# Gate and value products of the first two token blocks made in two halves of 128 tokens

## The chip, the cores and the metric

The kernel runs on one core of a Trainium2 chip, with float32 data throughout. The metric is the device time of one launch in microseconds (us): from the inputs in HBM to the output in HBM. The time before is the median of three runs.

## The reference

The attention has 8 batches, 8 heads, 576 tokens each and a head width of 64. Every query keeps its 32 largest scores. The attention's output, with the heads side by side, is the input x (4608 tokens by 512) of a SwiGLU feed-forward block.

```python
scores = scale * np.matmul(q, k.transpose(0, 1, 3, 2))
kth = np.partition(scores, -top_k, axis=-1)[..., -top_k:-top_k + 1]
scores = np.where(scores >= kth, scores, -1000000000.0)
attn = np.exp(scores - np.max(scores, axis=-1, keepdims=True))
attn = attn / (np.sum(attn, axis=-1, keepdims=True) + 1e-09)
attn_out = np.matmul(attn, v)
x = attn_out.transpose(0, 2, 1, 3).reshape(B * S, H * D)      # (4608, 512)
g = x @ w_gate                                                # (4608, 1536)
silu = g * (1.0 / (1.0 + np.exp(-g)))
return silu * (x @ w_val) @ w_out                             # (4608, 512)
```

## The kernel before

**Units.** The attention is cut into 160 units: for each batch b (8), for each query tile qt (four of 128 queries and a last one of 64), for each pair of heads hp (4). Units with qt = 4 are "short": they work on one row of 576 scores for each partition, the others on two. In this text the units are numbered 0 to 159, so that units 0 to 3 make the first 128 tokens of batch 0, units 4 to 7 the next 128, and units 16 to 19 are the first short ones. The main loop runs over the units, and each turn of it issues a step of several units: for unit n the top-32 search on VectorE (`select`: MAX8, L271, and MATCH_REPLACE8, L275, in alternation, and a threshold, L281); for unit n-1 the addition of the penalty on GpSimd (`penalize`, L291 and L293) and the exponentials on ScalarE (`weigh`, L302); for unit n-2 the normalisation (`normalize`, L312, L314, L317); for unit n-3 the transposes on TensorE (`turn`, L329, copied out at L330); for unit n-4 the product with the values (`values`, L349 and L358, copied into the tile `xT` at L373); for unit n+1 the scores (`scores`, L250, copied out at L255).

**Feed-forward blocks.** The 4608 tokens are also cut into 18 blocks of 256 (`BLK`). `values` fills the tile `xT[kb]` of a block and counts in `done[kb]` the columns that are there, summed over the four head pairs. `feed(kb)` is a generator of the work of one block. It makes 12 products, a gate and a value product for each of six pairs of columns tiles of the weights: a product is eight matmuls into one PSUM tile "f" (three buffers), at L412, and each shows as two instructions in the trace, so 16. ScalarE empties a gate product with three operations (L430 to L432) and a value product with one (L437), and GpSimd multiplies (L433, L438). Then come 24 matmuls of the second layer (L449) into `o_ps`. The generator yields after half a product, or after two matmuls of the second layer; what lies between two yields is a "piece", and a block has 24 + 12 = 36 pieces.

**Order and credits.** The order of the instructions on each engine is the order in which the program issues them; nothing is rearranged. Pieces are put between the steps of the units by a ledger: each unit adds 4.6 credits (2.3 where it is short) up to a limit of 8, a piece costs one, and `pieces(2)`, `pieces(1)`, `pieces(1)`, `pieces(6)` in each turn of the loop are the places where pieces may be issued. `piece()` starts a new block only when all of its 256 tokens are there. The work that ScalarE and GpSimd do on a product is put off: it waits in the lists `on_act` and `on_pool` until two have gathered or the loop empties them.

**Weights.** The three weight matrices are loaded and rounded to a shorter mantissa in 72 portions of 128 by 256 (`rounded`, `weights`): a DMA, two ScalarE operations (L101, L106), two on GpSimd (L103, L113) and two on VectorE (L110, L116). A call of `next(weight)`, here a "weight step", issues four different portions' stages at once, five, three, two and no steps behind the newest. The loop calls for five steps to every eleven VectorE operations, which makes four or five steps in a full unit. `need(n)` makes sure that the first n portions have been issued before a matmul that uses them, and calls for as many steps on the spot as are missing. The first 48 portions are those of w_gate and w_val, eight for each pair of products; 24 portions of w_out follow.

```python
    def need(n):
        while ready[0] < n:
            next(weight)
```

Of the kernel before, what the change touches and what calls it, by code (L numbers as in the profile page):

```python
# [8 lines left out]
AF = mybir.ActivationFunctionType  # L9
ALU = mybir.AluOpType  # L10
FP32 = mybir.dt.float32
# [4 lines left out]
P = 128  # L16
# [4 lines left out]
BLK = 256  # L21
# [6 lines left out]
def kernel(  # L28
# [27 lines left out]
    nc = tc.nc  # L56
# [5 lines left out]
    NHP = H // 2  # L62
    KC = DM // P
    MC = DFF // P
    MS = MC // 2
    NBLK = B * S // BLK
    scale = 1.0 / float(D) ** 0.5
# [8 lines left out]
    ffn = ctx.enter_context(tc.tile_pool(name="ffn", bufs=2))  # L76
# [11 lines left out]
    wg = consts.tile([P, KC, DFF], FP32, name="wg")  # L88
    wv = consts.tile([P, KC, DFF], FP32, name="wv")
# [31 lines left out]
    def weights():  # L121

        pieces = []
        for f in range(0, DFF, WP):
            for src, dst in ((w_gate, wg), (w_val, wv)):
                for c in range(KC):
                    pieces.append((src[c * P : (c + 1) * P, f : f + WP], dst[:, c, f : f + WP]))
        for c in range(MC):
            for f in range(0, DM, WP):
                pieces.append((w_out[c * P : (c + 1) * P, f : f + WP], wo[:, c, f : f + WP]))  # L130
        pieces = [rounded(*p) for p in pieces]
        lags = (5, 3, 2, 0)
        for n in range(len(pieces) + lags[0]):
            for lag in lags:
                if 0 <= n - lag < len(pieces):
                    next(pieces[n - lag], None)
            ready[0] = max(n - lags[0] + 1, 0)
            yield
# [8 lines left out]
# [4 lines that stand above are left out]
# [187 lines left out]
    xT, done = {}, {}  # L338
# [41 lines left out]
    def store(o, g0):  # L380

        at = g0
        while at < g0 + P:
            b, c = divmod(at, S)
            j, p0 = divmod(c, P)
            n = min(g0 + P - at, S - c, P - p0)
            r0 = b * S + (c if j == J else J * p0 + j)
            dst = out[r0 : r0 + n, :] if j == J else out[r0 : r0 + J * (n - 1) + 1 : J, :]
            nc.sync.dma_start(dst, o[at - g0 : at - g0 + n, :])
            at += n  # L390

    on_act, on_pool = [], []

    def flush(queue):
        while queue:
            queue.pop(0)()

    def feed(kb):

        x = xT.pop(kb)
        hs = []

        def product(w, s, then):
            ps = ps_f.tile([P, 2, BLK], FP32, tag="f", name="f")
            need(8 * s + (4 if w is wg else 8))
            for i in range(2):
                m = 2 * s + i  # L410
                for kc in range(KC):
                    nc.tensor.matmul(  # L412
                        ps[:, i, :],
                        w[:, kc, m * P : (m + 1) * P],
                        x[:, kc, :],
                        start=(kc == 0),
                        stop=(kc == KC - 1),
                    )
                if i == 1:
                    on_act.append(lambda: then(ps))  # L420
                yield

        for s in range(MS):
            h = ffn.tile([P, 2, BLK], FP32, tag="h", name="h", bufs=MS + 1)
            hs.append(h)


            def gate(ps, h=h):
                half = ffn.tile([P, 2, BLK], FP32, tag="gv", name="half_g", bufs=3)
                nc.scalar.activation(h[:], ps[:], AF.Tanh, scale=0.5)  # L430
                nc.scalar.mul(half[:], ps[:], 0.5)
                nc.scalar.add(h[:], h[:], 1.0)  # L432
                on_pool.append(lambda: nc.gpsimd.tensor_mul(h[:], h[:], half[:]))  # L433

            def value(ps, h=h):
                val = ffn.tile([P, 2, BLK], FP32, tag="gv", name="val", bufs=3)
                nc.scalar.copy(val[:], ps[:])  # L437
                on_pool.append(lambda: nc.gpsimd.tensor_mul(h[:], h[:], val[:]))  # L438

            yield from product(wg, s, gate)  # L440
            yield from product(wv, s, value)
        for t in range(BLK // P):
            ps = ps_f.tile([P, DM], FP32, tag="f", name="o_ps")
            for m in range(MC):
                need(8 * MS + 2 * m + 2)
                if m == 6:
                    flush(on_act)
                    flush(on_pool)
                nc.tensor.matmul(  # L449
                    ps[:],  # L450
                    hs[m // 2][:, m % 2, t * P : (t + 1) * P],
                    wo[:, m, :],
                    start=(m == 0),
                    stop=(m == MC - 1),
                )
                if m == MC - 1:

                    def finish(ps=ps, t=t):
                        o = ffn.tile([P, DM], FP32, tag="o", name="o")
                        nc.scalar.copy(o[:], ps[:])  # L460
                        store(o, kb * BLK + t * P)

                    on_act.append(finish)
                if m % 2 == 1:
                    yield

    NU = len(units)
    todo = list(range(NBLK))
    current = []

    def piece():

        if len(on_act) > 1:
            flush(on_act)
        if len(on_pool) > 1:
            flush(on_pool)
        while True:
            if not current:
                if not todo or done.get(todo[0], 0) < NHP * BLK:
                    return False  # L480
                flush(on_act)
                flush(on_pool)
                current.append(feed(todo.pop(0)))
            if next(current[0], 0) == 0:
                current.pop()
                continue
            return True

    def fetch(n):

# [5 lines left out]
            load(i + NHP)  # L496

    def pieces(n):
        for _ in range(n):
            if credit[0] >= 1 and piece():  # L500
                credit[0] -= 1

    def run(steps):
        for _ in steps:
# [14 lines left out]
    credit = [0.0]  # L519
# [4 lines left out]
    for n in range(NU + VALUES):  # L524
# [37 lines left out]
        if n < NHP:  # L562
            load_v(n)
        pieces(2)
        flush(on_act)
        flush(on_pool)
# [12 lines left out]
    while piece():  # L579
        pass  # L580
# [48 lines left out]
```

## Time and profile before

| | |
|---|---|
| median of three runs | 1912.69 us (1911.77 to 1916.11) |
| profiled execution, its own time | 1915.14 us |
| span of that execution, first to last instruction | 1913.4 us |
| TensorE (PE) matmul busy | 1756.5 us, 92% |
| TensorE weight load (PEld) busy | 1297.0 us, 68% |
| VectorE (DVE) busy | 1608.9 us, 84% |
| ScalarE (ACT) busy | 1156.3 us, 60% |
| GpSimd (POOL) busy | 816.0 us, 43% |
| mean granted TensorE clock | 0.959 |

A row of the trace's groups gives the line of the program, the engine, the operation, the tiles (output, arrow, inputs), the shapes and the count, then the union of their busy time, the mean duration of one in ns, and the idle time of the engine before them with what ended it. In a timeline a row is a run of like instructions: its start in us from the span's start, its length, and in brackets the idle time before it. In a table by stretches, a row gives the busy time and the count of instructions of each engine in that stretch, then the granted TensorE clock as a share of full speed. Matmuls are pipelined, so that the distance between the starts of two is what one costs, and not its listed duration.

### The profile page before, as it was taken

The page shows a single profiled execution, that of the slowest core. Times are in us where ns is not written, and L with a number is a line of the kernel's source. Part 1 is how long each engine was busy: PE and PEld are TensorE (multiplying, and loading weights), DVE is VectorE, ACT ScalarE, POOL GpSimd, SP SyncE. Part 2 cuts the span into 40 slices and gives each one's busy share as a digit, 9 for nine tenths or more (in the row PEclk, how much of TensorE's full clock was granted, in tenths as well). Part 3 has the DMA queues.
Part 4 walks back from the last instruction along what each step waited for, and adds up shares of the span by engine and source line. Part 5 has one row for each costly group of instructions (what it writes and reads, how often), then busy time and mean ns, then how long its engine had stood idle before and what let it go on. Part 6 is the DMA issues. An engine that isn't in the chain of part 4 may idle for free.

```text
span 1913.4 us, 29363 instructions
## 1 busy us (share of the span) xinstructions
PE 1756.5 (92%) x10144; PEld 1297.0 (68%) x10144; DVE 1608.9 (84%) x3476; ACT 1156.3 (60%) x2821; POOL 816.0 (43%) x846
## 2 busy tenths in 40 slices
PE   3437789989999999999999999999999999999999
PEld 2336558667677777676768676868686868586866
DVE  7999889998899979998799979999799989999400
ACT  5656656566666656675657566656675656665421
POOL 4566644335343525353335343525243535353412
PEclk7668899989999999999999999999999999999999
DMA  7322202000300012000210003000210001000000
GB/s 185 88 78 82 67 22 69 11 1 3 76 12 12 2 27 63 12 1 13 53 37 1 12 4 87 1 12 1 60 31 12 1 14 45 18 1 12 1 12 11
DMA packets 111253, 59.58 MB, mean 31 GB/s; under 512 B 89088, under 2 KB 97280, under 8 KB 111104
## 3 DMA queue, kind: packets, MB, share of 16 engines
q1 hardware_dynamic: 109904, 57.41, 11.5%
q8 instruction: 80, 1.31, 0.3%
q14 instruction: 69, 0.57, 0.1%
q10 hardware_dynamic: 1200, 0.30, 0.1%
HBM read 48.23 MB, written 9.44 MB: 30 GB/s over the span
## 4 chain that ended last, share of the span: by engine, by line
PE 82%; DVE 6%; POOL 5%; ACT 4%; issue 2%; DMA 0%; SPq 0%; POOLq 0%; DVEq 0%; ACTq 0%
PE f L412 38%; PE o_ps L449 19%; PE av L358 8%; PE etps L329 7%; PE s L250 7%; DVE m L271 2%; POOL e L293 2%; DVE rest L275 2%; PE s L236 2%; ACT e L302 1%; PE av L349 1%; PE kqps L205 1%; ACT sc L255 1%; POOL size L113 1%; POOL size L103 1%
## 5 line engine op out<-in xcount | busy, mean ns | idle before, releaser
L271 DVE MAX8 m<-rest 128x8 f32<-128x576 f32 x864 | 615.2, 747 | 2.2
L275 DVE MATCH_REPLACE8 rest<-m,rest 128x576 f32<-128x576 f32 x576 | 424.1, 743 | 0.0
L412 PE MATMUL f<-xT,wg 128*128 128x256 f32 x1728 | 407.5, 386 | 0.0
L293 POOL TENSOR_TENSOR e<-e,sc 128x1152 f32<-128x1152 f32 (+1 forms) x160 | 382.7, 2392 | 42.4 <-DVE e L281 38.8
L412 PE MATMUL f<-xT,wv 128*128 128x256 f32 x1728 | 395.8, 381 | 0.0
L449 PE MATMUL o_ps<-wo,h 128*128 128x512 f32 x864 | 387.6, 598 | 0.0
L412 PEld LDWEIGHTS f<-xT,wg 128*128 128x128 f32 x1728 | 324.2, 191 | 71.5 <-issue 29.9
L412 PEld LDWEIGHTS f<-xT,wv 128*128 128x128 f32 x1728 | 325.3, 190 | 53.3 <-issue 10.5
L433 POOL TENSOR_TENSOR h<-h,half_g 128x512 f32<-128x512 f32 x108 | 138.4, 1282 | 453.0 <-ACT h L432 435.0
L271 DVE MAX8 m<-sc 128x8 f32<-128x576 f32 x288 | 205.6, 750 | 123.9 <-ACT sc L255 78.8
L329 PE MATMUL etps<-ident,e 128*128 128x128 f32 (+1 forms) x1312 | 187.5, 288 | 125.9 <-POOL size L103 48.1
L449 PEld LDWEIGHTS o_ps<-wo,h 128*128 128x128 f32 x864 | 159.4, 190 | 193.1 <-issue 186.9
L329 PEld LDWEIGHTS etps<-ident,e 128*128 128x128 f32 (+1 forms) x1312 | 159.4, 147 | 176.1 <-POOL size L103 51.3
L330 ACT COPY et<-etps 128x512 f32<-128x512 f32 (+1 forms) x448 | 184.7, 482 | 148.5 <-PE etps L329 147.1
L302 ACT ACTIVATE e<-e,bias 128x576 f32<-128x576 f32 x288 | 222.1, 776 | 74.9 <-POOL e L293 74.5
L317 ACT ACTIVATE e<-e,tot 128x576 f32<-128x576 f32 x288 | 210.5, 780 | 5.4 <-DVE tot L314 5.1
L275 DVE MATCH_REPLACE8 rest<-m,sc 128x576 f32<-128x576 f32 x288 | 211.9, 742 | 0.0
L438 POOL TENSOR_TENSOR h<-h,val 128x512 f32<-128x512 f32 x108 | 139.7, 1293 | 149.6 <-ACT val L437 149.6
L250 PE MATMUL s<-kqT 64*128 64x288 f32 x1024 | 173.1, 446 | 9.6 <-ACT kqT L210 6.4
L312 POOL TENSOR_SCALAR tot<-tot 128x2 f32<-128x2 f32 (+1 forms) x160 | 37.4, 234 | 329.3 <-ACT e L302 320.9
L358 PE MATMUL av<-et,v 128*64 128x128 f32 (+1 forms) x2560 | 174.6, 282 | 0.0
L255 ACT COPY sc<-s 128x288 f32<-128x288 f32 x512 | 165.0, 410 | 2.5 <-PE s L250 2.5
(44 smaller groups left out, 1436.0 us busy)
## 6 DMA issues: line engine op xcount, KB each, us to landing
kq_in<-in_k_dram SPq DMA_DIRECT2D x64, 128.0 KB, 2.8
v<-in_v_dram SPq DMA_DIRECT2D x32, 256.0 KB, 3.0
kq_in<-in_q_dram SPq DMA_DIRECT2D x62, 128.0 KB, 3.1
w<-in_moe_w_gate_dram SPq DMA_DIRECT2D x24, 256.0 KB, 2.7
w<-in_moe_w_val_dram SPq DMA_DIRECT2D x24, 256.0 KB, 2.7
w<-in_moe_w_out_dram SPq DMA_DIRECT2D x24, 256.0 KB, 2.6
out_dram<-o SPq DMA_DIRECT2D x40, 128.0 KB, 2.4
out_dram<-o SPq DMA_DIRECT2D x16, 256.0 KB, 2.3
```

The lines of the kernel that those rows point to most:

```text
L250: nc.tensor.matmul(ps[:, 0:half], slab[d, q0 : q0 + P], slab[d, k0 : k0 + half])
L255: nc.scalar.copy(sc[:, i * half : (i + 1) * half], ps[:, 0:half])
L271: nc.vector.max(m[:, t, 8 * r : 8 * r + 8], cur[:, hs])
L275: nc.vector.match_replace(rest[:, hs], m[:, t, 8 * r : 8 * r + 8], cur[:, hs], LOWEST)
L293: nc.gpsimd.tensor_tensor(e[:, every], e[:, every], sc[:, every], ALU.add)
L302: nc.scalar.activation(e[:, hs], e[:, hs], AF.Exp, bias=bias[:, t : t + 1], scale=scale, accum_out=tot[:, t : t + 1],)
L317: nc.scalar.mul(e[:, hs], e[:, hs], tot[:, t : t + 1])
L329: nc.tensor.transpose(ps[0:kl, c * P : (c + 1) * P], e[:, k0 : k0 + kl], ident[:])
L330: nc.scalar.copy(et[0:kl, c0 : c0 + cn, :], ps[0:kl, 0 : cn * P].rearrange("p (c j) -> p c j", c=cn),)
L358: nc.tensor.matmul(av[hh * R : (hh + 1) * R, 0:ql], v_last[:, hh, :] if c == J else vt[:, hh, c, :], moving, start=last and c == 0, stop=c ...
L412: nc.tensor.matmul(ps[:, i, :], w[:, kc, m * P : (m + 1) * P], x[:, kc, :], start=(kc == 0), stop=(kc == KC - 1),)
L449: nc.tensor.matmul(ps[:], hs[m // 2][:, m % 2, t * P : (t + 1) * P], wo[:, m, :], start=(m == 0), stop=(m == MC - 1),)
```

## The change

For blocks 0 and 1 the tokens are taken in two halves of 128 columns. `feed` makes all 12 products of the first half as soon as the first 128 tokens are there, then waits (it yields 0) until the other 128 are there, makes the 12 products of the second half, and then the second layer as before. A half product is eight matmuls of 128 columns in place of 256, with the same weights; ScalarE and GpSimd work on half as many columns in each operation. A half product's pieces cost half a credit each. `piece()` now returns the size of what it issued, and starts a block when the first of its parts is there. Blocks 2 to 17 are made as before, with the same pieces.

```diff
+    def parts(kb):
+        return [slice(0, P), slice(P, BLK)] if kb < 2 else [slice(0, BLK)]
+
     def feed(kb):
-        x = xT.pop(kb)
+        x = xT[kb]
         hs = []
-        def product(w, s, then):
+        def product(w, s, c, then):
+            n = c.stop - c.start
             ps = ps_f.tile([P, 2, BLK], FP32, tag="f", name="f")
             need(8 * s + (4 if w is wg else 8))
             for i in range(2):
                 m = 2 * s + i
                 for kc in range(KC):
                     nc.tensor.matmul(
-                        ps[:, i, :],
+                        ps[:, i, 0:n],
                         w[:, kc, m * P : (m + 1) * P],
-                        x[:, kc, :],
+                        x[:, kc, c],
                         start=(kc == 0),
                         stop=(kc == KC - 1),
                     )
                 if i == 1:
-                    on_act.append(lambda: then(ps))
-                yield
+                    on_act.append(lambda: then(ps[:, :, 0:n], c))
+                yield n / BLK
-        for s in range(MS):
-            h = ffn.tile([P, 2, BLK], FP32, tag="h", name="h", bufs=MS + 1)
-            hs.append(h)
...
+        for c in parts(kb):
+            while done[kb] < NHP * c.stop:
+                yield 0
+            for s in range(MS):
+                if c.start == 0:
+                    hs.append(ffn.tile([P, 2, BLK], FP32, tag="h", name="h", bufs=MS + 1))
+                h = hs[s]
+                def gate(ps, c, h=h):
+                    half = ffn.tile([P, 2, BLK], FP32, tag="gv", name="half_g", bufs=3)
+                    hc, gc = h[:, :, c], half[:, :, c]
+                    nc.scalar.activation(hc, ps, AF.Tanh, scale=0.5)
+                    nc.scalar.mul(gc, ps, 0.5)
+                    nc.scalar.add(hc, hc, 1.0)
+                    on_pool.append(lambda: nc.gpsimd.tensor_mul(hc, hc, gc))
...
+                yield from product(wg, s, c, gate)
+                yield from product(wv, s, c, value)
+        del xT[kb]
...
     def piece():
...
-                if not todo or done.get(todo[0], 0) < NHP * BLK:
-                    return False
+                if not todo or done.get(todo[0], 0) < NHP * parts(todo[0])[0].stop:
+                    return 0
...
     def pieces(n):
-        for _ in range(n):
-            if credit[0] >= 1 and piece():
-                credit[0] -= 1
+        while n > 0 and credit[0] >= 1:
+            size = piece()
+            if not size:
+                break
+            n -= size
+            credit[0] -= size
```

More of the change, by code (lines that the diff above doesn't have):

```diff
@@ L419, in product, with value @@
                 if i == 1:
-                    on_act.append(lambda: then(ps))
-                yield
-        for s in range(MS):
-            h = ffn.tile([P, 2, BLK], FP32, tag="h", name="h", bufs=MS + 1)
-            hs.append(h)
[L428 to L441, printed above, removed]
+                    on_act.append(lambda: then(ps[:, :, 0:n], c))
[14 more added lines that the diff above has]
+                    on_pool.append(lambda: nc.gpsimd.tensor_mul(hc, hc, gc))
+                def value(ps, c, h=h):
+                    val = ffn.tile([P, 2, BLK], FP32, tag="gv", name="val", bufs=3)
+                    hc, vc = h[:, :, c], val[:, :, c]
+                    nc.scalar.copy(vc, ps)
+                    on_pool.append(lambda: nc.gpsimd.tensor_mul(hc, hc, vc))
+                yield from product(wg, s, c, gate)
+                yield from product(wv, s, c, value)
+        del xT[kb]
         for t in range(BLK // P):
@@ L464, in feed @@
                 if m % 2 == 1:
-                    yield
+                    yield 1
     NU = len(units)
@@ L483, in piece @@
                 current.append(feed(todo.pop(0)))
[L484 to L487, printed above, removed]
+            size = next(current[0], None)
+            if size is not None:
+                return size
+            current.pop()
     def fetch(n):
```

## The prediction

> **What bounds the kernel now.** I read the page's slices first, since the change touches the start alone.
>
> ```profile
> PE   3437789989999999999999999999999999999999
> ...
> DVE  7999889998899979998799979999799989999400
> ...
> PEclk7668899989999999999999999999999999999999
> ```
>
> A slice is 47.8 us. VectorE is full from the second slice, TensorE is at 3 to 4 tenths for three slices and full from the eighth or so. So TensorE has room at the start, and the last three slices are TensorE alone. The change can gain at the end only if it leaves fewer pieces for the end. I therefore counted the credit ledger through the loop, with the old code and the new.
>
> Before, block 0 starts in unit 11 (when unit 7's values are in) and block 1 in unit 20; both are finished in unit 27, units 28 to 30 issue none, and block 2 starts in unit 31 with the ledger at its limit of 8. After, unit 7 issues 7.5 credits (15 half pieces) and unit 8 the last 4.5 of the first half; units 9 and 10 wait; the second half is issued in units 11 and 12; block 1 starts in unit 15; all is finished in unit 25, and **unit 31 starts with the same 8 credits and the same work left, 28 pieces after the loop in both**. Nothing moves out of the tail: the 12 credits brought forward make units 26 to 30 idle for the feed-forward instead. What counts is how long units 7 to 30 take. The bounds of units are VectorE's first MAX8 of each, and the table by stretches gives units 7, 8, 9, 10, 11, 12, 13, 14, 15, then 16 to 19, 20 to 28 and 29 to 30:
>
> ```profile
> 109.99:124.81 14.82, 7.00 (x41) 5.22 (x39) 13.80 (x34) 9.04 (x24) 8.47 (x13) 0.64 0.29 80
> 124.81:138.37 13.56, 5.02 (x33) 4.43 (x35) 12.79 (x32) 8.39 (x22) 8.55 (x13) 0.62 0.30 93
> 138.37:152.94 14.57, 6.18 (x41) 4.78 (x37) 13.60 (x34) 9.03 (x24) 8.80 (x14) 0.65 0.28 86
> 152.94:167.04 14.10, 6.03 (x35) 4.90 (x35) 13.80 (x34) 9.14 (x24) 8.48 (x13) 0.64 0.29 86
> 167.04:183.32 16.28, 16.28 (x92) 14.25 (x91) 13.05 (x32) 10.85 (x26) 9.48 (x14) 1.00 0.22 73
> 183.32:203.13 19.81, 15.29 (x78) 12.00 (x74) 16.93 (x35) 12.74 (x33) 13.62 (x17) 0.83 0.20 58
> 203.13:219.40 16.27, 13.85 (x79) 10.84 (x77) 13.59 (x33) 10.39 (x27) 10.62 (x15) 1.00 0.24 77
> 219.40:237.36 17.96, 12.96 (x68) 9.70 (x67) 14.50 (x34) 11.27 (x28) 10.94 (x15) 0.88 0.21 62
> 237.36:253.26 15.90, 15.22 (x72) 10.00 (x71) 13.11 (x32) 8.46 (x21) 9.54 (x13) 0.92 0.02 4
> 253.26:283.42 30.16, 25.50 (x139) 14.36 (x139) 24.69 (x50) 16.40 (x41) 10.38 (x14) 0.94 0.11 29
> 283.42:384.15 100.73, 99.02 (x589) 72.38 (x587) 95.68 (x208) 63.90 (x159) 41.99 (x40) 1.00 0.15 39
> 384.15:405.27 21.12, 14.68 (x95) 11.46 (x97) 21.12 (x46) 14.51 (x36) 5.72 (x6) 0.72 0.00 1
> ```
>
> Columns: stretch, length, then PE, PEld, DVE, ACT, POOL busy with counts, clock. A full unit with nothing beside it takes 10.56 (units 29 and 30). With four or five weight steps it takes 13.6 to 14.8, some 0.85 a step (unit 7: 4.26/5). With weight steps and feed-forward pieces it takes 15.9 to 19.8, though TensorE and VectorE both have idle time in units 12 to 14. The waits of units 7 to 30 say on what:
>
> ```profile
> POOL size L113 <- DVE size L110: 21.0, 22, 1.8
> ...
> DVE size L110 <- POOL size L103: 18.1, 9, 3.5
> ```
>
> (us, times, longest.) VectorE and GpSimd wait for each other inside the weight rounding. Units 11 to 15 hold 15.0 of the 18.1: there ScalarE's and GpSimd's work on products is queued ahead of the rounding.
>
> **Part by part: TensorE.** A block's first layer becomes 24 half products of 16 instructions. TensorE's timeline prices one:
>
> ```profile
> 295.48 0.60 PE L205 MATMUL kqps<-ident,kq_in 128*128 128x128 f32 x4
> 295.92 3.62 PE L412 MATMUL f<-xT,wv 128*128 128x256 f32 x16
> 299.38 0.71 PE L329 MATMUL etps<-ident,e 128*128 128x128 f32 x5
> ```
>
> Start to start, 256 columns cost (299.38 - 295.92)/16 = 0.216, 128 columns, each with its own 128x128 weight load, (295.92 - 295.48)/4 = 0.110. A half product is 1.75 against 3.46 for a whole one: 48 x 1.75 - 24 x 3.46 = +1.0 us. Its far end is PEld's 0.190 mean for an f load, if loads were not overlapped: 48 x 16 x 0.08 = +61. I take 1.0: the 0.110 row loads as many weights for each matmul as the new one will. The Trainium skill ("TensorE: Matmul & The Clock Gate", LDWEIGHTS) speaks against narrow matmuls: a load takes the weight's columns over 1.2 GHz, 107 ns here, however few columns stream. By that rule 128 columns are the least width that still hides a load; had the loads to be paid on top, 768 x 0.107 would add 82 us (an estimate from that page). The 0.110 row agrees that they need not.
>
> **ScalarE and GpSimd.** The four emptying operations are doubled in number: starts of 128x512 ones lie 0.49 apart, of 128x256 ones (L101, L106) 0.33; 96 x 0.33 - 48 x 0.49 = +8.2 us of ScalarE. GpSimd's multiplications: 48 x 0.73 (L113, two inputs, 128x256) - 24 x 1.28 = +4.3. Both lie beside other work (ACT is busy 63.90 of 100.73 in units 20 to 28), so I cost them at nothing; with that cover gone, at most 12.5. That the second half's writes to `xT` might hold up matmuls on the first costs under 1 us, as those copies stand ahead of them on ScalarE anyway. No DMA is added; the 10 early weight loads queue on SP, at 2.7 us each to landing, six buffers ahead.
>
> **The weights.** Here the change adds a wait. Before, unit 11 finds 49 portions ready and `need` never forces a step. After, unit 7 ends with 35, and unit 8 needs 36, 40, 44 and 48: it **forces ten steps** (1, 4, 2 and 3) on top of its own four. All 42 steps from unit 7 on then end in unit 13 rather than 16. What is queued behind a forced step is the rest of the top-k search, on the same VectorE queue; TensorE's products wait too. Between two steps with nothing else to do the loop is L103 0.40, hand-over 0.1, L110 0.29, hand-over 0.15, L113 0.69: 1.63 us, of which VectorE works 0.54. How such a meeting looks with products about is in unit 12, VectorE and GpSimd side by side:
>
> ```profile
> 186.30 2.62 POOL L293 TENSOR_TENSOR e<-e,sc 128x1152 f32<-128x1152 f32 x1
> ...
> 188.88 1.45 POOL L438 TENSOR_TENSOR h<-h,val 128x512 f32<-128x512 f32 x1
> ```
>
> ```profile
> 186.76 2.44 DVE L116 SCALAR_TENSOR_TENSOR wo<-w,size 128x256 int32<-128x256 int32 x1
> 189.12 1.36 DVE L110 TENSOR_SCALAR size<-size 128x256 int32<-128x256 int32 x1
> ```
>
> L116 lasts 2.44 in place of 0.41, until L293 is done; L110 1.36 in place of 0.29.
>
> Unit 8 then goes so. VectorE's first four operations end at 2.8. The forced five come next; ScalarE reaches their L101 only after the exponentials (behind L293, which GpSimd's multiplications push to an end near 4.9) and the score copies, at 7.7 (L101 follows the first exponential by 2.7 in unit 7). The first step, then four emptying operations (1.3) and two multiplications (1.4) ahead of the second, bring VectorE to 12.0; two more loops and the last L110 to 15.3. The rest of the search is 10.56 - 2.8 = 7.8, nine steps' own VectorE time 9 x 0.54 = 4.9, and the five forced among them wait 1.1 each, with one more emptying ahead: 6. Together **34.0**, against 13.56. Bounds: 10.56 + 14 x 0.85 = 22.5 (the rate of unit 7) and 10.56 + 14 x 1.85 = 36.5 (the rate of unit 12).
>
> **The sum**, units 7 to 30. Unit 7: as unit 11 (16.28) with one step more (1.0): 17.3. Unit 8: 34.0. Units 9 and 10 as before: 14.6 and 14.1. Units 11 and 12 as before, with nearly the same credits: 16.3 and 19.8. Unit 13, ending the weights as unit 15 did: 15.9. Units 14 to 19 hold no weights now, 18 credits as before: TensorE's demand. A credit is 1.73; units 20 to 28 spent 37 of them in 99.0, so attention takes (99.0 - 64.0)/9 = 3.9 a unit; 18 x 1.73 + 6 x 3.9 = 54.5 (before: 64.0). Units 20 to 28 hold 25 credits in place of 37, so VectorE sets them: 9 x 10.56 = 95.0, say 96 (before 100.7). Units 29 and 30: 21.1. That is 303.6 against 295.3, **+8.3 us**: -14 where the weights have gone and feed-forward thins out, +23 in units 7 and 8. On the profiled execution's 1915.14 this gives 1923.4; that execution lies 2.45 above the median, and on 1912.69 it gives **1921.0**.
>
> **Rivals.** (1) *The forced steps hide*, as steps do in units 3 to 10, because half-width operations leave smaller lumps in GpSimd's queue. Place: units 8 and 12; price: 22.5 and 16.7 (without the 3.1 of the two long operations shown), 14.6 less than my sum: -6.3, 1906.4. It decides where unit 8 stays under 25.7. For it: unit 7's rate. Against: there VectorE always had top-k operations between the steps; the forced ones have none. (2) *PSUM buffers*: three "f" buffers now last 5.2 us of matmuls instead of 10.4, while ScalarE empties them at the same places in its order; TensorE then waits, and scores come late. Price: up to 2 us in each of units 7, 11 and 15 to 19, +14: 1935. Against: whole products met no such wait in unit 11. (3) *Weight loads exposed*: +61 less what units 7 to 13 hide, half of it: 1951. (4) *Nothing happens*, if the first half could not start early: excluded by the count of `done`, which is full for 128 tokens after unit 3's values.
>
> **How the numbers follow.** Mine 0.61, rival (1) 0.25, (2) 0.10, (3) 0.04. My own range: 27 to 36.5 for unit 8, and 49 to 58.8 for units 14 to 19 (units 34 to 39 took 58.8 with the same 18 credits): 1911 to 1928. The range reaches into rivals (1) and (2): 1908 to 1930. About 0.2% (3.8 us) is what a measurement can tell from no change. Faster by more: most of rival (1), 0.15. Within: the rest of (1) and my lower end, 0.17. Slower: 0.68.
>
> **What would show it.** Unit 8 near 34 us, with VectorE idle over 10 us in it, waiting for L103; L412's 128-column starts 0.110 apart; no L116 after unit 13; units 14 and 15 near 11; units 26 to 30 at 10.56; from unit 31 the same order and lengths. I am wrong if unit 8 stays under 26, if TensorE waits for ScalarE in unit 7, or if anything after unit 31 has moved by itself.

## The result: 8.9 us slower

The changed kernel has a median of 1922.98 us (1921.26 to 1924.17, six runs); the kernel before, in the same runs, 1914.07 (1911.77 to 1916.11). The ratio is 1.0046, with a 95% interval of 1.0034 to 1.0059. The profiled execution took 1922.71 us, with a span of 1920.9.

The page of the changed kernel, the same three rows of its slices:

```profile
PE   3465899879999999999899999999999999999999
...
DVE  7968898998899979998799979999799989999400
PEclk7686999979999999999999999999999999999999
```

TensorE is busier in the third slice (6 for 3) and less busy in the fourth (5 for 7), and the three slices at the end look as they did. The table by stretches, cut at the same units as before: 7, 8, 9, 10, 11, 12, 13, 14, 15, 16 to 19, 20 to 28 and 29 to 30:

```profile
111.05:128.66 17.61, 12.22 (x95) 11.33 (x94) 13.81 (x34) 10.97 (x31) 9.91 (x15) 0.89 0.24 69
128.66:165.55 36.89, 27.13 (x157) 23.75 (x158) 20.38 (x52) 21.45 (x58) 26.88 (x42) 0.69 0.34 106
165.55:180.12 14.57, 7.99 (x57) 6.38 (x53) 13.69 (x34) 9.30 (x25) 9.48 (x15) 0.75 0.27 86
180.12:194.23 14.11, 6.33 (x39) 5.17 (x35) 13.82 (x35) 9.16 (x24) 8.48 (x13) 0.64 0.28 82
194.23:210.13 15.90, 11.23 (x96) 10.76 (x96) 13.05 (x32) 10.21 (x29) 9.65 (x15) 1.00 0.25 74
210.13:230.95 20.82, 18.64 (x169) 16.83 (x168) 15.11 (x34) 14.57 (x41) 15.65 (x22) 1.00 0.13 44
230.95:243.63 12.68, 12.68 (x47) 6.28 (x47) 12.39 (x30) 6.04 (x15) 6.96 (x10) 0.87 0.01 2
243.63:254.19 10.56, 10.56 (x59) 5.91 (x53) 10.56 (x25) 6.15 (x15) 3.07 (x3) 1.00 0.06 25
254.19:264.75 10.56, 10.56 (x63) 6.75 (x59) 10.56 (x25) 6.05 (x16) 3.07 (x3) 1.00 0.07 26
264.75:293.72 28.97, 27.62 (x255) 23.38 (x255) 24.36 (x49) 20.23 (x56) 13.96 (x18) 1.00 0.09 22
293.72:393.06 99.34, 86.05 (x651) 65.83 (x651) 95.54 (x207) 63.95 (x171) 39.14 (x45) 0.94 0.15 38
393.06:414.18 21.12, 12.22 (x76) 9.85 (x74) 21.12 (x48) 11.84 (x30) 6.13 (x6) 0.66 0.00 0
```

Together 303.13 us against 295.28: +7.85 of the profile's +7.57. The reader is to see three things. Unit 8 is 36.89 us long, of which VectorE works 20.38. Units 13 to 15 have become short: the last weight steps end in unit 13, and units 14 and 15 hold none. Units 20 to 28 gained 1.4 us only, though they hold a third less feed-forward work; VectorE's busy time there (95.54) is nearly the whole.

VectorE's waits for L103 in units 7 to 30 of the changed kernel, then those of unit 8 alone, then its timeline in unit 8 at the first five forced steps (in brackets the idle time ahead):

```profile
DVE size L110 <- POOL size L103: 30.3, 15, 7.2
...
DVE size L110 <- POOL size L103: 16.5, 9, 7.2
```

```profile
131.44 0.84 DVE L116 SCALAR_TENSOR_TENSOR wg<-w,size 128x256 int32<-128x256 int32 x1
132.20 0.30 DVE L110 TENSOR_SCALAR size<-size 128x256 int32<-128x256 int32 x1
132.42 0.41 DVE L116 SCALAR_TENSOR_TENSOR wv<-w,size 128x256 int32<-128x256 int32 x1
140.02 0.29 DVE L110 TENSOR_SCALAR size<-size 128x256 int32<-128x256 int32 x1 [7.19 <-POOL size L103]
140.23 0.42 DVE L116 SCALAR_TENSOR_TENSOR wv<-w,size 128x256 int32<-128x256 int32 x1
143.08 0.29 DVE L110 TENSOR_SCALAR size<-size 128x256 int32<-128x256 int32 x1 [2.43 <-POOL size L103]
143.29 0.42 DVE L116 SCALAR_TENSOR_TENSOR wv<-w,size 128x256 int32<-128x256 int32 x1
144.69 0.29 DVE L110 TENSOR_SCALAR size<-size 128x256 int32<-128x256 int32 x1 [0.98 <-POOL size L103]
144.90 0.42 DVE L116 SCALAR_TENSOR_TENSOR wv<-w,size 128x256 int32<-128x256 int32 x1
146.30 0.29 DVE L110 TENSOR_SCALAR size<-size 128x256 int32<-128x256 int32 x1 [0.98 <-POOL size L103]
146.51 1.42 DVE L271 MAX8 m<-rest 128x8 f32<-128x576 f32 x2
```

Of the five steps the first (131.44) waits for nothing. The second waits 7.19 us for ScalarE and GpSimd to come to it; the third waits 2.43 while two multiplications stand ahead; then a step costs 144.69 - 143.08 = 1.61 us. The top-k search goes on at 146.51, 17.9 us into the unit, with four of its operations done.

### The profile page after: what moved, and what is told of

It reads as the page before. It is cut to its first block, busy times and chain, and to the rows that moved or that the text cites. A ratio compares the mean times of both kernels' runs of the same rounds, so it can differ in the third digit from the quotient of the medians.

```text
span 1920.9 us, 30236 instructions
## 1 busy us (share of the span) xinstructions
PE 1761.7 (92%) x10528; PEld 1313.8 (68%) x10528; DVE 1607.6 (84%) x3476; ACT 1162.3 (61%) x2869; POOL 821.4 (43%) x870
## 4 chain that ended last, share of the span: by engine, by line
PE 82%; DVE 7%; POOL 4%; ACT 4%; issue 2%; DMA 0%; SPq 0%; POOLq 0%; DVEq 0%; ACTq 0%
PE f L417 38%; PE o_ps L461 18%; PE av L358 7%; PE etps L329 7%; PE s L250 6%; DVE m L271 3%; DVE rest L275 3%; PE s L236 2%; POOL e L293 2%; PE av L349 1%; PE kqps L205 1%; ACT e L302 1%; POOL size L113 1%; ACT sc L255 1%; POOL size L103 1%
## 5 line engine op out<-in xcount | busy, mean ns | idle before, releaser
L417 PE MATMUL f<-xT,wv 128*128 128x256 f32 (+1 forms) x1920 | 406.8, 364 | 17.2 <-ACT half_g L441 10.1
L417 PE MATMUL f<-xT,wg 128*128 128x256 f32 (+1 forms) x1920 | 411.2, 365 | 2.6 <-DVE wg L116 2.6
L293 POOL TENSOR_TENSOR e<-e,sc 128x1152 f32<-128x1152 f32 (+1 forms) x160 | 383.2, 2395 | 64.3 <-DVE e L281 50.4
L417 PEld LDWEIGHTS f<-xT,wv 128*128 128x128 f32 x1920 | 338.7, 193 | 69.2 <-issue 11.9
L417 PEld LDWEIGHTS f<-xT,wg 128*128 128x128 f32 x1920 | 334.7, 192 | 68.4 <-issue 28.4
L443 POOL TENSOR_TENSOR h<-h,half_g 128x512 f32<-128x512 f32 (+1 forms) x120 | 141.4, 1178 | 442.2 <-ACT h L442 430.1
L449 POOL TENSOR_TENSOR h<-h,val 128x512 f32<-128x512 f32 (+1 forms) x120 | 142.0, 1183 | 159.0 <-ACT val L448 158.4
L312 POOL TENSOR_SCALAR tot<-tot 128x2 f32<-128x2 f32 (+1 forms) x160 | 37.4, 234 | 314.9 <-ACT e L302 304.3
```

What stands on the lines that cost most here:

```text
L293: nc.gpsimd.tensor_tensor(e[:, every], e[:, every], sc[:, every], ALU.add)
L417: nc.tensor.matmul(ps[:, i, 0:n], w[:, kc, m * P : (m + 1) * P], x[:, kc, c], start=(kc == 0), stop=(kc == KC - 1),)
```

## The experiments

In the table, units 7 to 30 of each kernel's one profiled execution are cut in three: 7 to 10 (where the half products come early), 11 to 18, 19 to 30. The time after the bar is the median of the timed runs, and the ratio is to the kernel before in the same runs. All kernels have the same 28 pieces left after the loop.

| kernel | 7-10 | 11-18 | 19-30 | median | ratio (95%) |
|---|---|---|---|---|---|
| before | 57.05 | 106.84 | 131.39 | 1914.07 | 1 |
| changed | 83.18 | 90.64 | 129.31 | 1922.98 | 1.0046 (1.0034-1.0059) |
| before, ten forced steps | 73.73 | 93.57 | 131.39 | 1916.66 | 1.0021 (1.0013-1.003) |
| changed, waits for weights | 67.42 | 105.41 | 130.97 | 1922.51 | 1.0045 (1.0031-1.0059) |
| before, 7 steps to 11 | 67.22 | 80.89 | 131.04 | 1916.09 | 1.0013 (1.0004-1.0022) |
| changed, 7 steps to 11 | 79.23 | 85.60 | 128.95 | 1931.11 | 1.0094 (1.0081-1.0107) |
| the same, limit of 4.6 | 76.19 | 87.25 | 128.95 | 1929.49 | 1.0079 (1.0066-1.0092) |
| before, longer distance | 53.95 | 98.69 | 130.89 | 1899.53 | 0.9929 (0.9916-0.9943) |
| changed, longer distance | 78.73 | 89.11 | 129.31 | 1909.29 | 0.9981 (0.9972-0.9989) |
| the same, waits for weights | 60.51 | 105.47 | 130.97 | 1911.79 | 0.9987 (0.9978-0.9996) |

**The forced steps alone.** The kernel before, with the ten steps called for in unit 8 and no early product.

```diff
         dve(2, beside=False)
+        if n == 8:
+            need(40)
...
+        if n == 8:
+            need(44)
         pieces(1)
...
+        if n == 8:
+            need(48)
         pieces(1)
```

> The kernel before, with the ten forced weight steps alone: in unit 8 the loop asks for portions 40, 44 and 48 at the places where the changed kernel's products do, and no product is made early. Theory (a forced step costs the round trip between VectorE and GpSimd, 1.6 us, because no top-k operation stands between two of them): unit 8 takes 30 to 33 us instead of 13.6, VectorE waits over 8 us in it for L103; the weights end in unit 13, which gives back some 17 in units 13 to 19; the whole is 1911 to 1918. Rival (steps are dear only where products of the feed-forward are queued between them on ScalarE and GpSimd): unit 8 takes 22 to 25 us at the 0.85 us a step of unit 7, and the whole is 1903 to 1907.

Measured 1916.66 us, and unit 8 in its table by stretches:

```profile
124.38:154.65 30.27, 7.21 (x35) 5.47 (x35) 19.48 (x53) 16.10 (x42) 19.86 (x33) 0.62 0.42 129
```

VectorE's waits in that unit:

```profile
DVE size L110 <- POOL size L103: 10.8, 9, 2.9
```

30.27 us with no product about, 16.7 more than without the ten steps, 10.8 of unit 8 spent waiting for L103: the rival's 22 to 25 is out, and the round trip is the price. But it is only part of the loss. Against its own start the burst costs 16.7 us in units 7 to 10 and brings 13.3 back in 11 to 18, because the weights are done three units sooner. The changed kernel loses 9.5 more in units 7 to 10 (unit 7: 17.61 for 14.81; unit 8: 36.89 for 30.27) and gains 5.0 more after them. By the medians the burst is 3.2 us of the 8.9 and the early products are the rest. The intervals in the table are too wide to say which share is the larger.

**More weight steps, so that nothing is forced.** The same edit to both kernels:

```diff
-                due[0] += 5 / 11 if beside else 0
+                due[0] += 7 / 11 if beside else 0
```

> The changed kernel, with seven weight steps to eleven VectorE operations in place of five, so that 50 portions are there by unit 8 and nothing is forced. Theory (the forced steps are the loss): unit 8 falls from 36.9 to 19 to 22 us, units 0 to 6 get 11 longer, the weights end in unit 11, and the whole is some 1908 (1904 to 1913), 15 under the changed kernel. Rival (the half products' own cost, twice as many operations on ScalarE and GpSimd and quicker use of three PSUM buffers, is the loss): unit 8 falls no lower than 28 and the whole stays within 5 us of 1923.

> The kernel before with the same seven steps to eleven. Theory: steps cost 0.85 us in units without feed-forward work and 1.4 to 2 with it, so moving 23 steps from units 11 to 16 into units 0 to 10 costs 20 and gives back 27: 1906 (1902 to 1912), and the difference to the changed kernel at this rate is within 4 us either way, since early products then neither force steps nor shorten what VectorE sets. Rival (halves' own cost): the changed kernel at this rate is at least 8 us slower than this one.

Both expectations failed; what came true is the rival's part of the second, that the two kernels at this rate lie 8 us or more apart. The changed kernel at this rate took 1931.11 us, 8 us more than without the edit, and the kernel before 1916.09 instead of 1906. Two errors of mine are in that. A step's price is not fixed: in units 3 to 6, without products, it was (57.28 - 4 x 10.56)/18 = 0.84 us at five to eleven and (66.73 - 42.24)/25 = 0.98 at seven. And my theory, that the forced steps are the loss, fell: with none forced, the early start still costs 79.23 - 67.22 = 12.0 us in units 7 to 10 and 2.6 more after them, 1931.11 against 1916.09. In unit 8 of the changed kernel at this rate ScalarE and VectorE read:

```profile
160.30 0.38 ACT L440 ACTIVATE h<-f 128x256 f32<-128x256 f32 x1 [0.79 <-PE f L417]
...
161.15 0.43 ACT L101 ACTIVATE size<-w 128x256 f32<-128x256 f32 x1
...
163.26 0.29 DVE L110 TENSOR_SCALAR size<-size 128x256 int32<-128x256 int32 x1 [7.82 <-POOL size L103]
```

The unit began at 148.31. ScalarE came to its first weight operation 12.8 us later, with emptying operations and their waits for TensorE ahead of it; in unit 8 of the kernel before at the same rate it took 5.7 (150.63, unit begun at 144.91). VectorE's waits for L103 in that unit are 8.4 us here and 2.2 there.

**Block 0 alone in halves.**

```diff
-        return [slice(0, P), slice(P, BLK)] if kb < 2 else [slice(0, BLK)]
+        return [slice(0, P), slice(P, BLK)] if kb < 1 else [slice(0, BLK)]
```

> The changed kernel with block 0 alone in halves, block 1 whole. Theory: unit 8 keeps its 36 to 37 us, as all ten forced steps are block 0's; block 1 then starts in unit 19 with 8 credits and units 14 to 28 take 141 to 146 us instead of 149: 1917 to 1921. Rival (halves' own cost): a fall by half of the loss with unit 8 shorter as well. If block 1's early start is worth something, this one is slower than 1923.

Measured 1923.07 us, ratio 1.0061 (1.0046 to 1.0076): not to be told from the changed kernel. The median lies 2 us above the expected 1917 to 1921. Unit 8 kept its length (37.41), as expected; units 14 to 28 took 151.2 us in the profile, not 141 to 146. There block 1 starts with eight credits at once, and unit 20 took 16.25, of which VectorE waited 5.6 for GpSimd's L312. The profile is of one of two executions that took 1930 and 1931 us, against 1922.0 to 1923.4 for the other four, so that its 151.2 may be longer than usual. By the medians the loss belongs to block 0, and block 1's halves cost about what they bring.

**PSUM buffers.** In unit 7 of the changed kernel TensorE waits for a free "f" buffer:

```profile
PE f L417 <- ACT half_g L441: 5.4, 1, 5.4
```

That was the second rival of the prediction. I put gate and value half products side by side in one buffer:

```diff
-            ps = ps_f.tile([P, 2, BLK], FP32, tag="f", name="f")
+            if w is wg or n == BLK:
+                bank[0] = ps_f.tile([P, 2, BLK], FP32, tag="f", name="f")
+            o = 0 if w is wg or n == BLK else n
+            ps = bank[0][:, :, o : o + n]
```

> The changed kernel, with the gate and the value half product of a pair side by side in one PSUM buffer, so that three buffers hold six half products as they held three whole ones. No operation is added or taken away. New theory (half products outrun the three PSUM buffers: TensorE waits 5.4 us in unit 7 for ScalarE, whose emptying is queued behind the unit's last weight step; the late products then stand before unit 8's transposes and scores, ScalarE comes late to its weight steps and VectorE waits 7.2 us): TensorE's 5.4 us wait goes, the 7.2 falls to 4 to 5, unit 8 falls from 36.9 to 33 to 35, units 12 and 21 by 1 to 2 each: 1915 to 1919. Rival (the number of emptying operations, twice as many, is what delays the rounding): unit 8 stays at 36 or more and the whole within 2 us of 1923.

> The changed kernel with seven weight steps to eleven VectorE operations and the shared PSUM buffer. Theory of the PSUM buffers: TensorE's 7.0 us wait in unit 7 goes, unit 8 falls from 26.9 to 19 to 22, units 16 to 21 by 3 to 5: 1918 to 1924 after 1931. Rival (number of operations): unit 8 stays above 25, the whole above 1928.

Both got worse: 1930.67 (1.0086, 1.0073 to 1.01) and 1938.31 (1.013, 1.0116 to 1.0144). TensorE's wait in unit 7 had gone altogether, and unit 8 fell from 36.89 to 35.95 only (at seven to eleven from 26.86 to 24.43). So that wait explains little of unit 8's length. The test is not a clean one: the edit brought a new wait of its own, where a value product waits until the gate product in the same buffer has been read, 2.4 us of it in unit 8 itself. TensorE's waits of that kind in units 7 to 30:

```profile
PE f L421 <- ACT half_g L445: 11.3, 8, 3.3
```

Units 18 to 23 became 9 us longer by it. For the question of the buffers after unit 17 these two runs say nothing.

**Bunching.** Seven to eleven again, with the first half spread evenly:

```diff
-            credit[0] = min(credit[0] + (4.6 if nh == 2 else 2.3), 8.0)
+            credit[0] = min(credit[0] + (4.6 if nh == 2 else 2.3), 4.6 if n < 11 else 8.0)
```

> The changed kernel with seven weight steps to eleven VectorE operations and the ledger's limit at 4.6 credits instead of 8 up to unit 10, so that the first half's 12 credits go 4, 4, 4 into units 7, 8, 9 in place of 7.5 and 4.5. Nothing is forced, no operation is added. Theory (bunching: what unit 7 leaves over stands ahead of unit 8's exponentials, score copies and weight steps in the order of ScalarE and GpSimd): units 7 to 10 together take 72 to 75 us, against 79.2 with the limit of 8 and 67.2 without early products; the whole 1924 to 1928. Rival (every early half product costs VectorE the same wherever it stands, 1 us a credit): units 7 to 10 stay at 78 to 80, the whole at 1931.

Units 7 to 10 took 76.2 us, between the two forecasts; the whole 1929.49. Of the 12 us that early products cost there, 3 come from their standing close together; 1.6 of the 3 reach the median, and its interval overlaps with that of the limit of 8. Spread out, they still cost 9.

**Halves by themselves**, in blocks 2 to 17, each started when whole.

```diff
-        return [slice(0, P), slice(P, BLK)] if kb < 2 else [slice(0, BLK)]
+        return [slice(0, P), slice(P, BLK)] if kb >= 2 else [slice(0, BLK)]
...
-                if not todo or done.get(todo[0], 0) < NHP * parts(todo[0])[0].stop:
+                if not todo or done.get(todo[0], 0) < NHP * BLK:
```

> Halves by themselves: blocks 2 to 17 in halves, each block started only when all its 256 tokens are there, blocks 0 and 1 whole; no early start, nothing forced. TensorE: 16 blocks x 24 half products x 16 instructions at 0.112 less 16 x 12 x 16 at 0.216, +24 us. Theory (ScalarE's and GpSimd's doubled operations lie beside other work): 1930 to 1945. Rival (the doubled operations delay scores and normalisation, as the 2.5 us that unit 21 lost): 40 us more on top, 1965 to 1990. If weight loads were exposed it would be some 490 us more, 2400.

Measured 1924.6, ratio 1.0053 (1.004 to 1.0067): +10 us for sixteen blocks, less than either theory. TensorE's timeline in this kernel, two half products and what follows:

```profile
600.06 1.95 PE L417 MATMUL f<-xT,wg 128*128 128x128 f32 x16
601.85 1.95 PE L417 MATMUL f<-xT,wv 128*128 128x128 f32 x16
603.64 1.15 PE L329 MATMUL etps<-ident,e 128*128 128x128 f32 x9
```

1.79 us for 16, 0.112 each: weight loads are hidden at 128 columns. Halves cost 0.6 us a block where no weight rounding is about, so by themselves neither their matmuls nor their doubled emptying operations are the loss. What the doubled operations cost in front of weight steps, this run does not show.

**Waiting for the weights instead of forcing them.**

```diff
-            need(8 * s + (4 if w is wg else 8))
+            while ready[0] < 8 * s + (4 if w is wg else 8):
+                yield 0
...
-                need(8 * MS + 2 * m + 2)
+                while ready[0] < 8 * MS + 2 * m + 2:
+                    yield 0
```

> The changed kernel with block 0's products waiting for their weights instead of forcing steps, all else as it is. Theory: unit 8 falls from 36.9 to 15 to 19, the weights end in unit 16 again, units 12 to 16 take back most of it because their weight steps now meet products again, and units 16 to 19 get block 0's second layer late: 1918 to 1924, little under the changed kernel. Rival (forced steps are all of the loss): at or below the kernel before, 1913.

Measured 1922.51, as expected: unit 8 fell to 18.55 and nothing was won, since the weight steps then stood in units 11 to 16 again (units 11 to 18 took 105.41 us, not 90.64). The rival's 1913 is out.

**A longer distance in the rounding.** One more step between GpSimd's L103 and VectorE's L110, in both kernels; `bufs` of one output tile pays for the two buffers.

```diff
-        size = conv.tile([P, n], FP32, tag="size", name="size", bufs=4)
+        size = conv.tile([P, n], FP32, tag="size", name="size", bufs=5)
-        ulps = conv.tile([P, n], I32, tag="ulps", name="ulps")
+        ulps = conv.tile([P, n], I32, tag="ulps", name="ulps", bufs=3)
-        lags = (5, 3, 2, 0)
+        lags = (6, 4, 2, 0)
-                        o = ffn.tile([P, DM], FP32, tag="o", name="o")
+                        o = ffn.tile([P, DM], FP32, tag="o", name="o", bufs=1)
```

> The changed kernel with one weight step more between GpSimd's clamp (L103) and VectorE's shift (L110), and one more buffer for each of the two tiles between them, paid for by one buffer less for the output tile. Theory (VectorE loses its time waiting for L103 of the step before, 30.3 us in units 7 to 30): in a forced group the round trip no longer sets the pace, a step falls from 1.6 to about 1.2 us (GpSimd's own 0.73 and 0.40); VectorE's waits for L103 fall below 15; unit 8 falls to 28 to 32: 1906 to 1914. Rival (ScalarE is late by a whole unit's products, more than a step can cover): unit 8 stays above 34 and the whole above 1919.

> The kernel before with the same longer distance. Its VectorE waits 18.1 us for L103 in units 7 to 16, all in five or six long waits. Theory: about half of it goes: 1903 to 1909. Rival (ScalarE's lateness): within 3 us of the kernel before.

> The changed kernel with the longer distance in the weight rounding, and with block 0's products waiting for their weights (yielding 0) instead of forcing steps. The first half then goes 7.5, 1.5, 2, 1 into units 7 to 10. Theory (forced steps and early products each cost): unit 8 falls from 34.9 to 14 to 17; block 0's second layer waits for w_out until unit 16; the whole lies between the two kernels with this distance, 1901 to 1907 (1909.3 and 1899.5). Rival (forced steps are all of the loss): 1899 or less.

The kernel before came down to 1899.53 us, 14 under itself and better than the expectation; it beats both kernels. VectorE's waits in its units 7 to 30:

```profile
DVE m L271 <- ACT sc L255: 7.8, 5, 2.7
DVE wo L116 <- POOL size L113: 3.2, 4, 1.1
DVE size L110 <- POOL size L103: 1.5, 5, 0.3
```

The 18.1 us on L103 have become 1.5, with 3.2 on the other hand-over. Part of the gain lies ahead of them: units 0 to 6, which hold no product, fell from 97.22 to 92.30.

The changed kernel with the same edit took 1909.29, within the expected 1906 to 1914. Its unit 8 did not fall to 28 to 32, though: 34.90. Eleven steps are forced there and not ten, since a portion is ready one step later. VectorE's waits in the unit fell from 16.5 us to 10.0, most of them now at the other end of the round trip, which the edit left as it was; and its busy time rose from 20.38 to 24.92, with many an L110 at 0.81 us and L116 at 0.61. From the waits of its units 7 to 30:

```profile
DVE wv L116 <- POOL size L113: 8.2, 4, 3.9
DVE wo L116 <- POOL size L113: 4.9, 2, 4.2
DVE size L110 <- POOL size L103: 3.7, 4, 2.9
```

So the change costs 9.8 us here too, and by the ratios about 11 where its products wait for their weights (1911.79, over the expected 1901 to 1907).

## Why the prediction was right

The time is 1922.98 for 1921.0, and the difference +8.9 for +8.3. The main mechanism was there: ten forced steps in unit 8, in which VectorE idles for 16.5 us, all of it waiting for L103. That the sum came so close is in part luck, as the terms show:

- **The ledger.** Unit 31 starts with the same work in both, and from there the two profiles run nearly alike: the distance at the start of unit 31, less the 1.05 us that this execution began later, is 7.85, and at unit 159 it is 6.25. Nothing was won at the end.
- **Weight loads.** 0.112 us between two matmuls of 128 columns, as the 0.110 row said. Rival (3) is out. The load time that the Trainium skill states ("TensorE: Matmul & The Clock Gate", LDWEIGHTS), 107 ns for 128 columns, lies just under that spacing.
- **Unit 7**: 17.61 for 17.3. **Unit 8**: 36.89 for 34.0. The first forced group ended at 17.9 us instead of 15.3: four half multiplications, and not two, stood ahead of L293 on GpSimd, it ended 6.8 us into the unit in place of 4.9, and ScalarE came to its first L101 at 10.4 in place of 7.7. The loop was 1.61 for 1.63, and the later five waits came to 4.9 us for 6.
- **Units 9 to 12**: within 1.0 us each.
- **Unit 13** 12.68 for 15.9, and **units 14 to 19** 50.1 for 54.5: I took attention as 3.9 us of TensorE a unit from the busy time of units 20 to 28, and 50.1 less 18 x 1.73 leaves 3.2. In units 14 and 15 VectorE was busy all of the 10.56 us too, so their length is not TensorE's alone. **Units 20 to 28** 99.3 for 96: unit 21, which holds half products of block 1, was 2.5 longer, and VectorE waited 1.9 of it for GpSimd's L312. These misses of -3.2, -4.4 and +3.3, with +2.9 in unit 8, nearly cancel, so the sum is better than its terms. The range has a slip: 27 for unit 8 and 49 for units 14 to 19 give a lower end of 1908.5, not 1911.
- **The cause.** The prediction laid unit 8's length to the forced steps, with the products as a part of each wait. The runs divide it otherwise: of 26.1 us lost in units 7 to 10, 16.7 are the burst and 9.5 the early products; of 18.3 gained later, 13.3 come with the burst. By itself the burst costs 3.2 us of 8.9 (by the ratio 1.0021, 4.0). Without any forced step the early start still lost 15 (seven to eleven), or as much as with them (waiting).
- **Where the expected gain went.** 11.5 credits, 11.5 x 1.73 = 19.9 us of TensorE work, left units 19 to 30 (27.5 in place of 39), and these became 2.1 us shorter (131.39 to 129.31): VectorE, busy 122.75 of the 129.31, sets them. The 12 credits of the first half arrived in units 7 and 8, among weight steps for which VectorE waits.
- **Rival (2)** was there: TensorE waited 5.4 us for ScalarE in unit 7, which the prediction had named as a sign of being wrong. The price it gave did not come, as unit 7 took 17.61 for 17.3, and the removal of the wait took 0.9 us off unit 8. Rival (1) is out.

Open is how the 9 to 12 us that the early products cost in units 7 to 10 divide between ScalarE's and GpSimd's order; no run took one of the two away alone. That these products' operations stand in front of the weight steps on both is read from the timelines, and not shown by a run.

## What to carry to other kernels

Work moved into an engine's idle time gains only if that engine sets the stretch that it is taken from; count first which one does. Where it lands, look at every in-order queue that it passes: here a product's short operations on two side engines stood in front of a round trip that the busiest engine waits for. Before adding work to such a place, lengthen the distance between the two ends of the round trip, which was worth 14 us by itself. It did not make the change cheaper: with it the early start still cost 9.8 us.

## What was not expected of the hardware

Beside GpSimd's multiplications some of VectorE's operations take longer and others do not: in unit 8 of the changed kernel L116 took 0.84 and 0.94 us beside them (131.44, 157.64) and 0.41 alone, L110 0.81 (156.91) and 0.29 alone, while a MATCH_REPLACE8 at 130.05, between 129.77 and 131.19 wholly beside two of them, kept its 0.73. The dearer weight step at seven to eleven, with the same operations, was not foreseen either.
